# Batch 1 of an attention-and-FFN kernel: its second score group one place earlier, its state read one place earlier, its two weight transposes next to each other

## The chip, the cores and the metric

The kernel runs on one core of one Trainium2 chip. The metric is device time in microseconds (us) of one execution; the kernel before takes 153.98 us (median of five runs, 153.81 to 155.08). A separate execution was profiled. All times on the profile's clock are us from the start of the profiled span.

A core has five engines, each with its own instruction stream that is worked off in order: TensorE (PE: matmuls, with weight loads on their own row, PEld), VectorE (DVE), ScalarE (ACT), GpSimd (POOL) and SyncE (SP). Streams wait for each other on semaphores only. PE writes its results to PSUM; ACT and DVE copy them from there to SBUF. DMAs are started from an engine's stream and then run on their own; the starts by POOL, which also convert float32 to bf16 on the way, form one queue, those by SP and ACT another.

## The reference, cut to what matters

x is (8, 8, 512, 64): 8 batches, 8 heads, 512 rows, 64 features. state is (8, 8, 32, 64): 32 state rows per head. Attention is computed both ways, and its result goes through a feed-forward layer whose hidden value is the largest of three products.

```python
scores = scale * np.matmul(x, state.transpose(0, 1, 3, 2))   # 512 x 32 per head
a = softmax(scores, -1)
xread = np.matmul(a, state)                                  # 512 x 64 per head
scores2 = scale * np.matmul(state, x.transpose(0, 1, 3, 2))
sread = np.matmul(softmax(scores2, -1), x)                   # 32 x 64 per head
tokens = concatenate([xread, sread], axis=2)                 # 8 x 544 tokens of 512 features
h = np.maximum(np.maximum(tokens @ w1, tokens @ w2), tokens @ w3)   # 768 hidden
out = h @ w_out
```

## The kernel before, in words

The state is folded into the weights: for each batch the kernel forms G = state x W (W is w1, w2 and w3 side by side), so that the first FFN product of the xread tokens is a x G, with the softmax weights a (4 heads of 32 states fill the 128 rows of a matmul; the 8 heads make two such groups, g = 0 for the even heads and g = 1 for the odd ones). The sread tokens are gathered in a tile of their own and go through the FFN at the end.

Per batch b the steps are these; the lines are those of the profile.

- `x_transpose(b, g, ...)` (L178, L182): x is transposed on PE, and copied to `xT`.
- `scores(b, g0, g1)` (L200, L205): 8 matmuls per group into a PSUM tile `psh` and one exponential on ACT into `e`.
- `softmax(b, g0, g1, ...)` (L213, L215, L220): row sums `den` and reciprocals `rden` on DVE, then the product `a` on POOL.
- `sread(b)` (L267, L276, L278): 32 small matmuls of `e` with x into the PSUM tile `psr`, and two DVE operations, `rd` and `sr`.
- `a_transpose(b, g, copy)` (L231, L232): 4 PE transposes of `a` into the PSUM tile `pat`, and a copy to `aT` by the engine that is named, ACT or DVE.
- `g_cols(b, ms)` (L327, L333): for each 128 hidden columns m, 8 matmuls of a 64x32 block of the state with a slice of W, packed side by side in the array, into a PSUM tile `pg`, and an ACT copy to `G`. With `defer` the ACT copy is put off until after the `t` copy of the next `x_maxout`.
- `x_maxout(b, m)` (L377, L382, L385, L386): 6 matmuls (three products, two head groups each) into three PSUM tiles `pw`, an ACT copy `t` of the first, a DVE maximum `t` with the second, and a DVE maximum `ht` with the third.
- `ffn_out(b, j)` (L416, L419): 6 matmuls with w_out, an ACT copy, and a DMA to the output.

PSUM is kept in two rings: `two`, two tiles of two banks (`pg` among others), and `pw`, four tiles of one bank. `pw`, `psh`, `pxt` (the x transposes), `psr` and `pat` all take the next tile of the second ring in the order in which they are written down, so a step waits until the tile four places before it was read.

The schedule is written out by hand: the order of the calls is the order in each engine's stream. Batches 0 and 1 are woven into each other at the start, while the loads still run; from batch 2 on a loop places the steps of the next batch between the `x_maxout` steps of this one.

W is loaded by POOL in four slices of hidden columns (m = 0; m = 1; m = 2 and 3; m = 4 and 5), each in three parts, one per weight matrix (`load_w(c, parts)`, L109). All matmuls of `g_cols` for a column need all three parts of its slice. Between the calls that this document deals with POOL's stream holds, in this order: the product `a` of batch 1's group 0, the second part of the last slice, the product `a` of batch 1's group 1, the last part of the last slice (`load_w(3, (2,))`), the cast of states 2 and 3 to bf16 (L136, tile `st`), the loads of x of batch 2 (L70), of w_out (L471), of the other states (L58), of x of batches 3 and 4, and some fills. SP's stream holds, behind that cast, the DMA that transposes these states (L144, `stT`).

Of the kernel before, what the change touches and what calls it, by code (L numbers as in the profile page):

```python
# [15 lines left out]
def kernel(  # L16
# [14 lines left out]
    nc = tc.nc  # L31
# [10 lines left out]
    J = 4  # L42
# [11 lines left out]
    dve, act, pool = nc.vector.tensor_copy, nc.scalar.copy, nc.gpsimd.tensor_copy  # L54


    def load_st(k, eng):
        eng.dma_start(  # L58
            out=st_f[k],
            in_=state[2 * k:2 * k + 2].rearrange("b h n d -> (b h n) d").rearrange("(p t) d -> p t d", t=4))  # L60
# [38 lines left out]
    def m_cols(t, m):  # L99
        c = [m0 <= m < m1 for m0, m1 in chunks].index(True)  # L100
        f = (m - chunks[c][0]) * 128
        return w_slices(t, c)[:, :, :, f:f + 128]
# [27 lines left out]
    def bd(b, h):  # L130
        return bds[b // 2][:, b % 2, h]
# [18 lines left out]
    def states_place(k, copy):  # L150
        for c in range(2):
            r = slice(64 * c, 64 * c + 64)
            copy(out=bds[k][r, :, :, c, :].rearrange("p b h (q t) -> p (b h) q t", t=4),  # L153
                 in_=stT[k][r].rearrange("p t (k q) -> p k q t", q=8))
# [8 lines left out]
    def new(d, b, shape, name, bufs=2):  # L163
        d[b] = work.tile(shape, BF16, tag=name, bufs=bufs, name=name)
# [23 lines left out]
    def scores(b, g0, g1):  # L188
        n = g1 - g0
        if g0 == 0:  # L190
            new(e, b, [128, J, 2, HS, Ns], "e")
        if n == 2:
            p = pp.tile([128, J, n, HS, Ns], F32, tag="two", name="ps")
        else:
            p = pp.tile([128, J, n, HS, Ns], F32, tag="pw", bufs=4, name="psh")
        for jj in range(2):
            for g in range(g0, g1):
                for s in range(HS):
                    h = 2 * s + g
                    nc.tensor.matmul(  # L200
                        p[:, 2 * jj:2 * jj + 2, g - g0, s, :], xT[b][:, h, jj, :],
                        bd(b, h).rearrange("p c n -> p (c n)"),
                        start=(g == g0 and s == 0 and (n == 2 or jj == 0)),
                        stop=(g == g1 - 1 and s == HS - 1), skip_group_check=True)
        nc.scalar.activation(out=e[b][:, :, g0:g1], in_=p, func=AF.Exp, scale=scale)  # L205

    def softmax(b, g0, g1, *parts):

        n = g1 - g0
        if g0 == 0:  # L210
            new(a, b, [128, J, 2, HS, Ns], "a")
        den = work.tile([128, J, n, HS], F32, tag=f"den{n}", name="den")
        nc.vector.reduce_sum(out=den, in_=e[b][:, :, g0:g1], axis=AX.X)  # L213
        rden = work.tile([128, J, n, HS], F32, tag=f"rden{n}", name="rden")
        nc.vector.reciprocal(out=rden, in_=den)  # L215
        j0 = 0
        for mul, nj in parts:
            r = slice(j0, j0 + nj)
            j0 += nj
            mul(  # L220
                out=a[b][:, r, g0:g1].rearrange("p j g s n -> p j (g s) n"),
                in0=e[b][:, r, g0:g1].rearrange("p j g s n -> p j (g s) n"),
                in1=rden[:, r].rearrange("p j g s -> p j (g s)").unsqueeze(3).to_broadcast((128, nj, n * HS, Ns)))

    def a_transpose(b, g, copy):

        if g == 0:
            new(aT, b, [128, J, 2, 128], "aT", bufs=3)
        p = pp.tile([128, J, 128], BF16, tag="pw", bufs=4, name="pat")
        for j in range(J):  # L230
            nc.tensor.transpose(p[:, j, :], a[b][:, j, g].rearrange("p s n -> p (s n)"), ident)  # L231
        copy(out=aT[b][:, :, g, :], in_=p)  # L232
# [17 lines left out]
    def sread(b):  # L250


        padded = b >= 2
        p = pp.tile([128, 2, 2 * D], F32, tag="pw", bufs=4, name="psr")
        for j in range(J):
            for g in range(2):
                for s in range(HS):
                    h = 2 * s + g
                    if padded:
                        c0 = (2 * h + j // 2) * PW + 1 + (D + 1) * (j % 2)  # L260
                        cols = x_pads[b % 2][:, c0:c0 + D + 1]
                        c = slice(j % 2, D + 1 + j % 2)
                    else:
                        xj = xv[b][:, h, j, :]
                        cols = bass.AP(xj.tensor, xj.offset, (xj.ap[0], (XW - (h * J + j) * D, 2), (1, D)))
                        c = slice(0, 2 * D)
                    nc.tensor.matmul(  # L267
                        p[32 * s:32 * s + 32, g, c], e[b][:, j, g, s, :], cols,
                        start=(j == 0 and g == 0), stop=(j == J - 1), skip_group_check=True,
                        tile_position=(0, 32 * s))  # L270
        den, c = p[:, :, D:D + 1], slice(0, D)
        if padded:
            den, c = work.tile([128, 2, 1], F32, tag="rs", name="rs"), slice(1, D + 1)
            nc.vector.reduce_sum(out=den, in_=p[:, :, 0:D + 2:D + 1], axis=AX.X)
        rd = work.tile([128, 2, 1], F32, tag="rd", name="rd")
        nc.vector.reciprocal(out=rd, in_=den)  # L276
        sr = work.tile([128, 2, D], BF16, tag="sr", bufs=B, name="sr")
        nc.vector.tensor_mul(out=sr, in0=p[:, :, c], in1=rd.to_broadcast((128, 2, D)))  # L278
        late.append(lambda: nc.sync.dma_start_transpose(
            out=ats[:, b].rearrange("p s n -> p (s n)"), in_=sr.rearrange("p g d -> p (g d)")))  # L280
# [4 lines left out]
    def flush_copies():  # L285
        while copies_due:
            copies_due.pop(0)()
# [30 lines left out]
    def g_cols(b, ms, copies=(act, act), defer=(False, False)):  # L318
        flush_copies()
        for m, copy, wait in zip(ms, copies, defer):  # L320
            if m == 0:
                new(G, b, [128, 2, NM * 384], "G", bufs=3)
            p = pp.tile([128, 2, 512], F32, tag="two", name="pg")
            pv = p[:, :, 0:384].rearrange("p g (i f) -> p g i f", i=3)
            for s in range(HS):
                for g in range(2):
                    nc.tensor.matmul(  # L327
                        pv[32 * s:32 * s + 32, g], bd(b, 2 * s + g)[64 * g:64 * g + 64, g, :],
                        m_cols(w_sb, m)[64 * g:64 * g + 64, s],
                        start=True, stop=True, tile_position=(64 * g, 32 * s))  # L330

            def place(m=m, pv=pv, copy=copy):
                copy(out=m_cols(G[b], m), in_=pv)  # L333

            if wait:
                copies_due.append(place)
            else:
                place()
# [27 lines left out]
    def maxout(b, m, n, lhs, rhs, nk, mid=None):  # L366


        if m == 0:
            new(ht, b, [128, NM, n], "ht", bufs=4)  # L370
        pw = []
        for k0, k1 in ((0, nk),) if mid is None else ((0, 1), (1, nk)):
            for i in range(3):
                if k0 == 0:
                    pw.append(pp.tile([128, 512], F32, tag="pw", bufs=4, name=f"pw{i}"))
                for k in range(k0, k1):
                    nc.tensor.matmul(pw[i][:, 0:n], lhs(i, k), rhs(k), start=(k == 0), stop=(k == nk - 1))  # L377
            if k1 < nk:
                mid()
        t0 = work.tile([128, 512], BF16, tag="t0", name="t0")  # L380
        t1 = work.tile([128, 512], BF16, tag="t1", name="t1")
        nc.scalar.copy(out=t0[:, 0:n], in_=pw[0][:, 0:n])  # L382
        if copies_due:
            copies_due.pop(0)()
        nc.vector.tensor_max(t1[:, 0:n], t0[:, 0:n], pw[1][:, 0:n])  # L385
        nc.vector.tensor_max(ht[b][:, m, :], t1[:, 0:n], pw[2][:, 0:n])  # L386

    def x_maxout(b, m, mid=None):
        maxout(b, m, 512,
               lambda i, k: m_cols(G[b], m)[:, k, i],  # L390
               lambda k: aT[b][:, :, k, :], 2, mid)
# [68 lines left out]
    load_w(3, (1,))  # L460
    x_maxout(0, 0, lambda: x_transpose(1, 1, dve))
    load_st(1, nc.scalar)
    g_cols(0, (1,))
    g_cols(1, (0,), defer=(True,))
    scores(1, 1, 2)
    softmax(1, 1, 2, (nc.gpsimd.tensor_mul, J))
    load_w(3, (2,))
    states_cast(1, pool)
    states_transpose(1, True)
# [8 lines left out]
    for k in range(1, B // 2):  # L478
        nc.gpsimd.memset(bds[k], 0.0)
    states_place(1, pool)  # L480
    x_maxout(0, 1)
    sread(1)
    a_transpose(1, 0, act)
    g_cols(1, (1,))
    a_transpose(1, 1, dve)
    x_maxout(1, 0, lambda: None)
    g_cols(0, (2, 3), defer=(False, True))
    x_maxout(1, 1)
# [97 lines left out]
```

## Time and profile before

| | us |
|---|---|
| five timed runs | 153.81, 153.88, 153.98, 154.55, 155.08 |
| profiled execution: its own time | 154.74 |
| its span, first to last instruction | 152.9 |
| PE busy | 144.6 (95% of the span) |
| ACT busy | 94.0 (61%) |
| DVE busy | 97.8 (64%) |
| POOL busy | 66.5 (43%) |
| wait of PE for a part of W's second slice | 0.97, from 14.15 to 15.12 |
| wait of PE for the ACT copy of that slice's G (batch 0) | 0.42, up to 16.39 |
| wait of PE for `a` of batch 1, group 1 | 0.13, up to 19.17 |

How to read it. The page gives busy times per engine and a table of groups of like instructions. The timeline gives the instructions of a stretch: start, length, engine, line, operation, written and read tiles, shape, how many, and in square brackets the idle time before and what ended it. Two instructions of one engine may overlap by about 0.1 us, since the next starts while the last one drains. The chain of waits goes back from the last instruction to what released each step. Matmuls are pipelined: their lengths overlap, and what counts is the distance from one start to the next.

### The profile page before, as it was taken

To read this page: it belongs to the slowest core of one execution; us is meant where nothing else is said; L and a number is where in the kernel's file an instruction comes from. 1 tells how busy PE (TensorE), PEld (TensorE's weight loads), DVE (VectorE), ACT (ScalarE), POOL (GpSimd) and SP (SyncE) were. 2 spreads that over 40 slices of the span, in tenths; PEclk is the share of its full clock that TensorE was granted. 3 is DMA by queue.
4 is the path that set the end of the run, shared out by engine and by line. 5 is a ranking of instruction groups with operands and counts; after the bars stand their busy time and mean duration, and the time that the engine had idled before them with its cause. 6 is when DMAs were issued, how large, how long until landed. Compare 5 with 4: busy or idle time off the path is not lost.

```text
span 152.9 us, 3474 instructions
## 1 busy us (share of the span) xinstructions
PE 144.6 (95%) x1366; PEld 70.6 (46%) x1382; DVE 97.8 (64%) x177; ACT 94.0 (61%) x145; POOL 66.5 (43%) x80
## 2 busy tenths in 40 slices
PE   6987899999999999999999999999999999999990
PEld 2544443554453445344534453445344556665450
DVE  3488668768827685768576867776767684566010
ACT  3654788686848656865686568656865637332440
POOL 8998499836421782078307310821082100100410
PEclk9999999999999999999999999999999999999998
DMA  4999999999938999999585953071206120210473
GB/s 117 192 180 188 208 161 111 198 234 196 252 63 176 149 181 281 173 120 180 188 185 77 191 165 137 6 201 41 110 13 198 43 107 0 81 58 0 163 253 137
DMA packets 37520, 21.85 MB, mean 143 GB/s; under 512 B 22528, under 2 KB 35072, under 8 KB 37504
## 3 DMA queue, kind: packets, MB, share of 16 engines
q0 software_dynamic: 17184, 14.94, 54.2%
q1 hardware_dynamic: 20032, 6.43, 23.2%
q10 hardware_dynamic: 288, 0.26, 0.6%
q8 instruction: 11, 0.18, 0.5%
q14 instruction: 5, 0.04, 0.1%
HBM read 15.20 MB, written 8.91 MB: 158 GB/s over the span
## 4 chain that ended last, share of the span: by engine, by line
PE 82%; POOL 5%; DMA 5%; ACT 2%; issue 2%; DVE 1%; POOLq 0%; DVEq 0%
PE pw L377 43%; PE po L416 28%; DMA w<-in_moe_w_dram 5%; PE pg L301 4%; POOL w L109 2%; PE ps L200 2%; POOL x L80 2%; PE pg L327 1%; PE psr L267 1%; ACT G L333 1%; PE ph L408 1%; ACT t L382 1%; POOL a L220 1%; DVE t L385 0%; DVE den L213 0%
## 5 line engine op out<-in xcount | busy, mean ns | idle before, releaser
L377 PE MATMUL pw<-aT,G 128*128 128x512 bf16 x288 | 69.2, 379 | 0.4 <-ACT G L333 0.4
L385 DVE TENSOR_TENSOR t<-t,pw 128x512 bf16<-128x512 bf16 (+1 forms) x54 | 35.1, 649 | 29.0 <-ACT t L382 28.5
L416 PE MATMUL po<-wout,ht 128*128 128x512 bf16 x183 | 46.4, 379 | 1.0 <-DVE t L385 0.2
L377 PEld LDWEIGHTS <-G 128*128 128x128 bf16 x288 | 26.8, 98 | 32.0 <-issue 2.9
L386 DVE TENSOR_TENSOR ht<-t,pw 128x512 bf16<-128x512 bf16 (+1 forms) x54 | 35.5, 658 | 5.6
L382 ACT CAST t<-pw 128x512 bf16<-128x512 f32 (+1 forms) x54 | 30.5, 565 | 12.0 <-PE pw L377 11.2
L419 ACT COPY osb<-po 128x512 f32<-128x512 f32 x33 | 19.3, 586 | 28.5 <-PE po L416 28.5
L416 PEld LDWEIGHTS <-ht 128*128 128x128 bf16 x198 | 18.8, 98 | 24.0 <-issue 2.8
L430 POOL DMA_DIRECT2D out_dram<-osb x14 | 7.9, 567 | 47.8 <-ACT osb L419 42.0
L220 POOL TENSOR_TENSOR a<-e,rden 128x1024 bf16<-128x1024 bf16 (+2 forms) x10 | 15.3, 1533 | 26.3 <-DVE rden L215 16.7
L308 ACT CAST G<-pg 128x1024 bf16<-128x1024 f32 x24 | 24.5, 1021 | 2.3 <-PE pg L301 1.6
L246 POOL COPY xp<-x 128x2048 bf16<-128x2048 bf16 x6 | 11.3, 1883 | 0.0
L213 DVE TENSOR_REDUCE den<-e 128x32 f32<-128x1024 bf16 (+1 forms) x10 | 10.0, 997 | 2.0 <-ACT e L205 2.0
L333 ACT CAST G<-pg 128x768 bf16<-128x768 f32 x11 | 8.8, 808 | 2.6 <-PE pg L327 2.6
L109 POOL DMA_DIRECT2D w<-in_moe_w_dram x12 | 9.2, 782 | 0.3 <-DMA x<-in_x_dram 0.3
L377 PE MATMUL pw<-ats,w 128*128 128x256 bf16 x72 | 8.7, 272 | 0.0
L205 ACT ACTIVATE e<-ps 128x1024 bf16<-128x1024 f32 x6 | 6.2, 1029 | 3.7 <-PE ps L200 3.7
L377 PEld LDWEIGHTS <-w 128*128 128x128 bf16 x72 | 7.1, 98 | 1.9
L301 PE MATMUL pg<-w,bd 64*32 64x512 bf16 x192 | 7.5, 381 | 0.0
L127 PE MATMUL idle<-zero 128*128 128x512 bf16 x15 | 5.5, 506 | 1.3 <-DVE zero L85 1.2
L153 POOL COPY bd<-stT 64x512 bf16<-64x512 bf16 x6 | 6.5, 1079 | 0.6 <-DMA stT<-st 0.4
L200 PEld LDWEIGHTS <-xT 128*128 128x128 bf16 x128 | 4.9, 98 | 2.1 <-issue 0.3
(61 smaller groups left out, 85.7 us busy)
## 6 DMA issues: line engine op xcount, KB each, us to landing
out_dram<-osb POOLq DMA_DIRECT2D x14, 512.0 KB, 3.5
x<-in_x_dram POOLq DMA_DIRECT2D x6, 512.0 KB, 9.2
w<-in_moe_w_dram POOLq DMA_DIRECT2D x6, 256.0 KB, 6.8
x<-in_x_dram POOLq DMA_DIRECT2D x3, 256.0 KB, 6.2
w<-in_moe_w_dram POOLq DMA_DIRECT2D x6, 128.0 KB, 6.4
wout<-in_moe_w_out_dram POOLq DMA_DIRECT2D x1, 768.0 KB, 11.4
out_dram<-osb SPq DMA_DIRECT2D x3, 256.0 KB, 2.0
x0f<-in_x_dram SPq DMA_DIRECT2D x1, 512.0 KB
```

The costliest lines, as they stand in the source:

```text
L109: nc.gpsimd.dma_start(out=w_slices(w_sb, c)[:, :, i, :], in_=w[:, :, m0 * 128:m1 * 128])
L220: mul(out=a[b][:, r, g0:g1].rearrange("p j g s n -> p j (g s) n"), in0=e[b][:, r, g0:g1].rearrange("p j g s n -> p j (g s) n"), in1=rden[: ...
L246: nc.gpsimd.tensor_copy(out=x_pads[b % 2][:, 2:2 + 2 * H * PW].rearrange("p (k c) -> p k c", c=PW)[:, :, 0:2 * D], in_=x_sb[b][:, 0:XW].re ...
L301: nc.tensor.matmul(ps[g][32 * s:32 * s + 32], bd(b, 2 * s + g)[64 * g:64 * g + 64, g, :], w_sb[64 * g:64 * g + 64, s, c0:c1], start=True, ...
L308: copy(out=G[b][:, :, c0:c1], in_=p[:, :, 0:n])
L333: copy(out=m_cols(G[b], m), in_=pv)
L377: nc.tensor.matmul(pw[i][:, 0:n], lhs(i, k), rhs(k), start=(k == 0), stop=(k == nk - 1))
L382: nc.scalar.copy(out=t0[:, 0:n], in_=pw[0][:, 0:n])
L385: nc.vector.tensor_max(t1[:, 0:n], t0[:, 0:n], pw[1][:, 0:n])
L386: nc.vector.tensor_max(ht[b][:, m, :], t1[:, 0:n], pw[2][:, 0:n])
L416: nc.tensor.matmul(p, ht[b][:, m, j * 128:(j + 1) * 128], wout_sb[:, m, :], start=(m == 0), stop=(m == NM - 1))
L419: act(out=o[:, j, :], in_=p)
```

## The change

Three calls of batch 1 change their place, and one copy its engine.

1. `scores(1, 1, 2)` and `softmax(1, 1, 2, ...)` stand ahead of `g_cols(0, (1,))` and `g_cols(1, (0,))`, the two pieces of G that read W's second and first slice, and no longer behind them. On PE these are 8 matmuls that pass 16; on ACT the exponential passes the copy of `G` for batch 0, m = 1. On DVE, POOL and SP nothing passes anything by this.
2. `sread(1)` stands ahead of `x_maxout(0, 1)`, and no longer behind it: its 32 matmuls pass 6 on PE, and its two DVE operations pass the two maxima.
3. `a_transpose(1, 1)` stands right behind `a_transpose(1, 0)`, ahead of the piece `g_cols(1, (1,))`, and its copy is made by ACT and no longer by DVE: on PE 4 transposes pass 8 matmuls, DVE has one copy less, ACT one more.

The streams of POOL and SP hold the same instructions in the same order. The tiles of the `pw` ring are dealt in the new order.

```diff
     x_maxout(0, 0, lambda: x_transpose(1, 1, dve))
     load_st(1, nc.scalar)
+    scores(1, 1, 2)
+    softmax(1, 1, 2, (nc.gpsimd.tensor_mul, J))
     g_cols(0, (1,))
     g_cols(1, (0,), defer=(True,))
-    scores(1, 1, 2)
-    softmax(1, 1, 2, (nc.gpsimd.tensor_mul, J))
     load_w(3, (2,))
     states_cast(1, pool)
     states_transpose(1, True)
...
     states_place(1, pool)
+    sread(1)
     x_maxout(0, 1)
-    sread(1)
     a_transpose(1, 0, act)
+    a_transpose(1, 1, act)
     g_cols(1, (1,))
-    a_transpose(1, 1, dve)
     x_maxout(1, 0, lambda: None)
```

`x_maxout(1, 0, lambda: None)` is the form in which the three matmuls of head group 0 stand ahead of the three of group 1, so that only the last three need `aT` of group 1.

## The prediction

> **What bounds the kernel now.** I read the page's busy lines first, to see which engine fills the span.
>
> ```profile
> PE 144.6 (95%) x1366; PEld 70.6 (46%) x1382; DVE 97.8 (64%) x177; ACT 94.0 (61%) x145; POOL 66.5 (43%) x80
> ```
>
> PE is busy for 95% of the span, so only what shortens PE's idle time, or its work, can pay. The change leaves PE's work alone. Next the waits of PE, from 21 us to the end:
>
> ```profile
> PE pg L327 <- ACT G L333: 0.3, 1, 0.3
> PE po L416 <- DVE t L385: 0.2, 1, 0.2
> ```
>
> Behind 21 us PE waits only twice, each time for engines that PE itself feeds, and never for a DMA. So all that PE wins by 21 us should reach the end, unless a load becomes late. Third, the chain of waits in the stretch that the diff touches:
>
> ```profile
> 7.71 7.37 DMA w<-in_moe_w_dram
> 15.07 0.04 issue
> 15.12 0.40 PE pg L327 x8
> ...
> 15.54 0.80 ACT G L333
> 16.34 0.51 ACT e L205
> ...
> 18.07 1.05 POOL a L220
> ...
> 19.17 0.40 PE pat L231 x4
> ```
>
> The third part of W's second slice lands at 15.07 and releases the pieces of G; behind them come the copy of G, the exponential of batch 1's odd heads, its sums, its product, its transposes. The scores need nothing of W: they hang on this load by their place only. Last the timeline, PE first and then the others:
>
> ```profile
> 13.33 0.81 PE L377 MATMUL pw<-aT,G 128*128 128x512 bf16 x3
> 15.12 0.52 PE L327 MATMUL pg<-w,bd 64*32 64x384 bf16 x16 [0.97 <-DMA w<-in_moe_w_dram]
> 15.57 0.41 PE L200 MATMUL psh<-bd,xT 128*128 128x64 bf16 x8
> 16.39 1.47 PE L377 MATMUL pw<-aT,G 128*128 128x512 bf16 x6 [0.42 <-ACT G L333]
> 17.79 0.63 PE L267 MATMUL psr<-x,e 128*32 128x128 bf16 x32
> 18.35 0.40 PE L231 MATMUL pat<-ident,a 128*128 128x128 bf16 x4
> 18.68 0.36 PE L327 MATMUL pg<-w,bd 64*32 64x384 bf16 x8
> 19.17 0.40 PE L231 MATMUL pat<-ident,a 128*128 128x128 bf16 x4
> 19.42 1.46 PE L377 MATMUL pw<-aT,G 128*128 128x512 bf16 x6
> ```
>
> ```profile
> 13.84 0.63 DVE L182 COPY xT<-pxt 128x1024 bf16<-128x1024 bf16 x1
> 15.16 0.69 DVE L386 TENSOR_TENSOR ht<-t,pw 128x512 bf16<-128x512 bf16 x1
> 16.23 0.60 ACT L205 ACTIVATE e<-psh 128x512 bf16<-128x512 f32 x1
> 18.07 1.04 POOL L220 TENSOR_TENSOR a<-e,rden 128x512 bf16<-128x512 bf16 x1 [2.19 <-DVE rden L215]
> 18.79 0.59 ACT L232 COPY aT<-pat 128x512 bf16<-128x512 bf16 x1 [0.47 <-PE pat L231]
> 19.60 0.42 DVE L232 COPY aT<-pat 128x512 bf16<-128x512 bf16 x1
> ```
>
> The reader is to see two holes on PE, 0.97 and 0.42 us, with 0.41 us of scores and 0.63 us of state reads standing behind them.
>
> **The change, part by part.** The point to compare is the end of batch 1's first maxout group on PE, now 19.42 + 1.46 = 20.88, since all behind it keeps its order.
>
> *Scores into the first hole.* They need `xT`, whose copy ends at 13.84 + 0.63 = 14.47. A release costs 0.05 (from 15.07 to 15.12), so they start at 14.52 and end 0.41 later, at 14.93, 0.14 ahead of the load. The exponential runs from 14.97 to 15.57. The copy of G started at 15.54. ACT starts the next instruction 0.1 before the last one ends (the exponential at 16.23, the copy's end at 16.34), so it could take this copy from 15.47: no loss. PE's next maxout group then stays at 16.39. The cover is thin: an exponential later by more than 0.07 delays that group one for one.
>
> *Softmax.* DVE is free at 15.16 + 0.69 = 15.85. With the old distances (sums at 16.87, product at 18.07 to 19.11) the product would run from 17.05 to 18.09, 1.02 earlier.
>
> *State read into the second hole.* Its 32 matmuls start behind the pieces of G, at about 15.57 where the scores stood, and end at 15.62 + 0.63 = 16.25, once the exponential is in. That is before 16.39, so they cost nothing; covered by the wait for the copy of G, and 0.56 (17.79 to 18.35) if that wait were gone. Its `rd` and `sr` come behind the reciprocals on DVE, which end at 16.89, and end near 17.4, before DVE's next maximum can start (the ACT copy `t` ends at 17.62).
>
> *Transposes.* The maxout group ends its issue at 17.79 as now; the first transposes start there rather than at 18.35, and are done at 18.19. The second ones wait for the product: 18.09 + 0.05 = 18.14. Then the 8 matmuls of G 0.33 later (18.35 to 18.68), at 18.47. ACT's deferred copy of G runs from 17.52 to 18.32, so the first `aT` copy runs from 18.22 to 18.81, the second 0.48 behind it (18.79 to 19.27 was the distance), from 18.70 to 19.29.
>
> *What is late next.* The next maxout group can start at 18.81 + 0.05 = 18.86. Its second PSUM tile is the one that `ht` of the group before still reads: `t` starts at 17.65 on DVE and `ht` 0.79 behind it (the distance in later pairs, 21.11 to 21.90), ending at 19.13, so the second matmul starts at 19.18. The other four follow by 0.216 each (1.46 less 0.38, over five). The sixth starts at 20.04 and ends at 20.42. The group's second half needs `aT` by 19.61 and has it at 19.34. So 20.88 becomes 20.42: **0.46 us won**.
>
> *The moved copy.* ACT takes 0.59 for what DVE did in 0.42. The slower copy lies 0.27 off the path; ACT's next copies, of G at 19.18 and of `t` at 20.0, still meet theirs. If that cover were gone it would cost 0.17.
>
> *Queues.* POOL's issues behind the product, and SP's transpose of the states behind POOL's cast, come up to 1.02 earlier. The cast's input lands at 13.76 + 5.0 = 18.76, the cast would start at 18.85, so it holds nothing up. The last part of W was issued at 19.07 and landed 5.7 later, at 24.8; its reader stands at 25.88, now at 25.42. The load of x of batch 2 landed at 28.6, its reader's weight load stands at 29.17, now 28.71: enough even if that load gained nothing. w_out (21.31 + 11.4 = 32.7) is read at 34.08, now 33.6. From both sides: between nothing (all loads ahead of need, as the waits behind 21 us say) and, in the nearest row of a late load, the wait of 0.97. I take nothing.
>
> The Trainium skill, page "DMA: Bandwidth & Descriptors", section "Anatomy of one DMA — SWDGE (gpsimd) path", gives a POOL-issued transfer about 2.0 us and its bytes over 436e3; for 256 KB that is an estimate of 2.6 us, against the 5.7 measured here. By it the last part of W would be there near 20.7, and the sum would still be 0.46. The same page, "SWDGE vs HWDGE vs iDMA", says that the two kinds of queue are served in turn, which speaks against moving the state transpose nearer to the W loads; by it alone the sum would only shrink, by an amount that the page doesn't give. The row behind that:
>
> ```profile
> 22.00:23.00 1.00, 1.00 (x6) 0.41 (x5) 1.00 (x2) 1.00 (x3) 1.00 (x3) 1.00 1.57 200
> 23.00:24.00 1.00, 1.00 (x6) 0.29 (x3) 0.90 (x3) 0.82 (x2) 1.00 (x2) 1.00 1.31 51
> ```
>
> The last column is GB/s: it falls from 200 to 51 a few us behind the issue of the transpose.
>
> Sum: the profiled execution, 154.74 (span 152.9 and 1.84 around it), would be 154.28. The median of the timed runs lies 0.76 below it; less 0.46 it is **153.5**.
>
> **The rivals.** *W's second slice lands earlier in the timed runs.* For it: the profiled run is 0.76 slower than the median, and in this stretch every step of before hangs on the landing at 15.07; against it: the time could as well be lost around the span. If it lands at L, the old end moves with it, 20.88 - (15.07 - L). The new one stops moving at L = 15.0, where ACT's exponential holds the copy of G: 20.35. They meet at L = 14.54. Below that the change loses; at L = 14.1, when PE is only just free (its last matmul starts at 13.77), it loses 0.44: 154.4. This is the slower mechanism with the weaker price.
>
> *The state transpose starves the last part of W.* For it: the fall to 51 GB/s, now 1.02 earlier and so over that load. Against it: the load is also issued 1.02 earlier, and in the old order landed amid the transposes. The new order loses nothing until 25.42, and ends slower than before from a landing at 25.88. Say it is held until the transposes' traffic ends, about 25.1 (an estimate: the transpose lands 28.2 now, its traffic is over near 26), and that half of the part ahead of it and all of its own are still to move, at the 1.3 per part that lie between landings now: it lands at 27.0, a stall of 1.6, net 1.1 slower, 155.1.
>
> *Timed runs wait for loads that the profile shows as early.* For it: two of five runs are 0.6 and 1.1 slower than the rest; against it: no such wait behind 21 us. Then the loads' 1.02 counts where PE's 0.46 does: 153.0.
>
> *The scores don't fit.* If `xT` were late by over 0.14, the pieces of G wait for them, at most their 0.41: 153.5 to 153.9.
>
> **How the numbers follow.** I take 0.5% (0.77 us) as what a measurement here can tell from no change. The forecast, with the misfit of scores within it, gets 0.55, at 153.1 to 153.9 (own range); a fifth of that lies below 153.21. Loads that were late: 0.15, faster. An early W slice: 0.15, nearly all within 0.5%. A starved last part: 0.15, two thirds of it beyond 154.75, and I give 0.03 more to slower for the early slice with the copy's 0.17 on top. Faster 0.11 + 0.15 = 0.26; slower 0.10 + 0.03 = 0.13; within 0.61. The range of 152.8 to 154.7 takes in the loads' gain with 0.2 to spare, the early slice to its end, and the milder part of the starved load.
>
> **What would show it.** Right: scores on PE at about 14.5, the wait for W at about 0.2 or less, state reads inside the wait for the copy of G, the product ending near 18.1, the maxout group of batch 1 ending near 20.4, and the same two small waits later. Wrong: the copy of G behind a late exponential; a PE wait for w at 25 or for x at 29; `t` copies later than their matmuls by more than before. It would be wrong altogether if the landing at 15.07 is not what the timed runs have, or if the moved loads collide.

## The result and the profile after

The changed kernel takes 154.29 us (median of 54 runs, 153.9 to 155.17). The kernel before, run many more times beside it, takes 154.18 us (94 runs, 153.4 to 156.05). The ratio is 1.0012, with a 95% interval of 1.0004 to 1.0020: slower by 0.06 to 0.31 us, where 0.46 us of gain was forecast. Runs more than 1.5% above the fastest run of the same kernel are left out of the ratios here and below, which leaves three of six and five of nine runs of the two kernels with a late slice.

The profiled execution of the changed kernel took 154.72 us, its span is 152.8. On the page PE is as busy as before, and DVE has given one copy to ACT:

```profile
PE 145.0 (95%) x1366; PEld 70.7 (46%) x1382; DVE 97.3 (64%) x176; ACT 94.4 (62%) x146; POOL 66.2 (43%) x80
```

The waits of PE from 21 us to the end are those of before, one for one:

```profile
PE pg L327 <- ACT G L333: 0.3, 1, 0.3
PE po L416 <- DVE t L385: 0.2, 1, 0.2
```

The timeline of PE in the stretch of the change (start, length, operation, shape, count, idle time before):

```profile
13.72 0.81 PE L377 MATMUL pw<-aT,G 128*128 128x512 bf16 x3
14.91 0.41 PE L200 MATMUL psh<-bd,xT 128*128 128x64 bf16 x8 [0.38 <-DVE xT L182]
15.25 0.52 PE L327 MATMUL pg<-w,bd 64*32 64x384 bf16 x16
15.70 0.88 PE L267 MATMUL psr<-x,e 128*32 128x128 bf16 x32
16.70 1.47 PE L377 MATMUL pw<-aT,G 128*128 128x512 bf16 x6
18.00 0.83 PE L231 MATMUL pat<-ident,a 128*128 128x128 bf16 x8
18.76 0.36 PE L327 MATMUL pg<-w,bd 64*32 64x384 bf16 x8
19.16 1.46 PE L377 MATMUL pw<-aT,G 128*128 128x512 bf16 x6
```

Batch 1's first maxout group ends at 19.16 + 1.46 = 20.62, 0.26 before the old 20.88. But there is no wait for W any more, for a reason that has nothing to do with the change: W's second slice is there early. The DMA view gives, for that load's third part, issued at 7.85, 6.5 us to landing (14.36); in the profile of before it was issued at 7.71 and took 7.4 (15.07). And PE came to the place 0.39 later than in the profile of before, because x of batch 0 had landed later (6.82 against 6.46). The scores now wait for `xT`, and the chain of waits in this stretch starts there and no longer at a load:

```profile
14.31 0.56 DVE xT L182
14.86 0.05 issue
14.91 0.42 PE psh L200 x8
15.33 0.02 issue
15.35 0.60 ACT e L205
15.95 0.70 ACT G L333
16.65 0.05 issue
16.70 0.62 PE pw L377 x2
```

The reader is to see the copy of G behind the exponential: it starts at 15.85, 0.1 before the exponential ends, though its slice has been there since 14.36.

```profile
15.85 0.79 ACT L333 CAST G<-pg 128x768 bf16<-128x768 f32 x1
```

A second thing is in the timeline of DVE. One maximum near 32 us starts 0.51 after the instruction before it, and not 0.11 after it as its twin did before (32.22, behind an end at 32.12). First before, then after:

```profile
31.44 0.68 DVE L385 TENSOR_TENSOR t<-t,pw 128x512 bf16<-128x512 bf16 x1
32.22 0.69 DVE L386 TENSOR_TENSOR ht<-t,pw 128x512 bf16<-128x512 bf16 x1
```

```profile
31.17 0.68 DVE L385 TENSOR_TENSOR t<-t,pw 128x512 bf16<-128x512 bf16 x1
32.36 0.69 DVE L386 TENSOR_TENSOR ht<-t,pw 128x512 bf16<-128x512 bf16 x1 [0.51 <-PE pxt L178]
```

Its two inputs were ready: `t` at 31.85, and the last matmul of its `pw` group at 31.02. The bracket names the x transposes on PE, which end at 32.21, since they are the last thing that ended before it. But the maximum does not need them: its twin before starts at 32.22 while they run until 32.48 (31.86 + 0.62). PE's maxout group behind it takes 1.64 instead of 1.46 (the transposes and that group on PE, first before, then after):

```profile
31.86 0.62 PE L178 MATMUL pxt<-ident,x 128*128 128x128 bf16 x8
32.32 1.46 PE L377 MATMUL pw<-aT,G 128*128 128x512 bf16 x6
```

```profile
31.59 0.62 PE L178 MATMUL pxt<-ident,x 128*128 128x128 bf16 x8
32.05 1.64 PE L377 MATMUL pw<-aT,G 128*128 128x512 bf16 x6
```

So 0.26 won at 20.6 are 0.09 at 34.0 (34.08 before, 33.99 now).

Two questions follow. Does W's second slice land near 15.1, or is that a chance of one execution? And whose is the 0.17 at 32 us?

Three numbers of each profile answer them. *Lateness*: from the end of the copy of `xT` of batch 1's odd heads to the landing of the third part of W's second slice. *Front*: from that end of the copy to the end of batch 1's first maxout group. *Tail*: from there to the end of the span.

### The profile page after: what moved, and what is told of

Same layout as the page of the kernel before. It is cut to its first block, busy times and chain, and to the rows that moved or that the text cites. A ratio compares the mean times of both kernels' runs of the same rounds, so it can differ in the third digit from the quotient of the medians.

```text
span 152.8 us, 3476 instructions
## 1 busy us (share of the span) xinstructions
PE 145.0 (95%) x1366; PEld 70.7 (46%) x1382; DVE 97.3 (64%) x176; ACT 94.4 (62%) x146; POOL 66.2 (43%) x80
## 4 chain that ended last, share of the span: by engine, by line
PE 84%; ACT 4%; DVE 4%; DMA 4%; issue 2%; POOL 0%; POOLq 0%; DVEq 0%
PE pw L377 44%; PE po L416 28%; PE pg L301 4%; DMA x<-in_x_dram 4%; PE ps L200 2%; PE psr L267 1%; ACT G L333 1%; DVE den L213 1%; PE pg L327 1%; ACT e L205 1%; ACT t L382 1%; PE ph L408 1%; DVE a L220 1%; PE pxt L178 1%; PE psh L200 1%
## 5 line engine op out<-in xcount | busy, mean ns | idle before, releaser
L127 PE MATMUL idle<-zero 128*128 128x512 bf16 x15 | 6.1, 547 | 1.3 <-DVE zero L85 1.2
```

## The experiments

Each ratio is against the kernel before in the same session.

**Both kernels once more.** No edit.

> The kernel before, profiled once more. Theory A (landing): the landing of W's second slice at 15.07 in the first profile is a chance of that execution; most executions have it near 14.4, as the profile of the changed kernel has (14.36). Then this profile shows the slice landing at 14.2 to 14.6, PE's wait for it at 0.3 us or less, and batch 1's first maxout group ending on PE near 20.3 and not at 20.88. Theory B (lost later): the landing is near 15.1 in each execution of before, the hole of about 1 us is there again, the group ends near 20.9, and what the change wins by then is lost behind it. Time: the same as before, ratio 0.998 to 1.002, under both.

> The changed kernel, profiled once more, beside the kernel before. Under theory A its group end does not follow the landing of the slice below 15.0: near 20.4 to 20.7 wherever the slice lands, set by the copy of xT, the exponential and then the copy of G. Under theory B the group ends near 20.4 and a PE wait of 0.2 to 0.5 us appears behind it that before does not have. Ratio to before 1.000 to 1.003 under both.

Before again: 154.19 us, ratio 1.0016 (1.0001 to 1.0032) to the same program in that session; the interval just misses one, which shows what a thousandth is worth here. So it is not certain that the changed kernel, at 1.0012, is truly slower; it is certain that the forecast gain of 0.46 us (0.003) is absent. Its PE timeline:

```profile
13.09 0.81 PE L377 MATMUL pw<-aT,G 128*128 128x512 bf16 x3
14.48 0.52 PE L327 MATMUL pg<-w,bd 64*32 64x384 bf16 x16 [0.58 <-DMA w<-in_moe_w_dram]
14.93 0.41 PE L200 MATMUL psh<-bd,xT 128*128 128x64 bf16 x8
15.76 1.47 PE L377 MATMUL pw<-aT,G 128*128 128x512 bf16 x6 [0.42 <-ACT G L333]
```

The slice lands at 14.44, lateness 0.23 where the first profile had 0.60; the hole is 0.58 and not 0.97, and the group ends at 20.25. I had expected at most 0.3 of hole under the landing theory, so this profile lies between the two theories; it shows that the 15.07 did not repeat. The changed kernel again: 154.40 us, ratio 1.0021 (1.0000 to 1.0043), lateness 0.24, front 5.77, exactly as in its first profile at a lateness of -0.49. In this second profile the slice lands at 14.98, nearly as late as the 15.07, but the copy of `xT` ends late too, at 14.74: what counts is the one against the other. Its tail is 132.20, that of before 132.01.

**The scores alone.**

```diff
     load_st(1, nc.scalar)
+    scores(1, 1, 2)
+    softmax(1, 1, 2, (nc.gpsimd.tensor_mul, J))
     g_cols(0, (1,))
     g_cols(1, (0,), defer=(True,))
-    scores(1, 1, 2)
-    softmax(1, 1, 2, (nc.gpsimd.tensor_mul, J))
```

> Only the scores and their softmax stand ahead of the pieces of G; the state read and the transposes stay where before has them. Theory A: with the slice there at 14.4 the scores delay the copy of G by their exponential, about 0.5 us, the state read's 0.6 us comes behind the maxout group again, and the earlier product ends no wait: slower than before by 0.3 to 0.8 us, ratio 1.002 to 1.005. Theory B: the hole takes the scores, the maxout group starts as before, the product's wait of 0.13 goes: faster or the same, ratio 0.997 to 1.000.

154.67 us, ratio 1.0045 (1.0027 to 1.0062). Slower, as the landing theory has it. PE's wait for the copy of G, 0.42 before, is 0.93 here, and the state read stands behind it as before:

```profile
14.49 0.52 PE L327 MATMUL pg<-w,bd 64*32 64x384 bf16 x16
15.94 1.47 PE L377 MATMUL pw<-aT,G 128*128 128x512 bf16 x6 [0.93 <-ACT G L333]
17.34 0.63 PE L267 MATMUL psr<-x,e 128*32 128x128 bf16 x32
```

Front 6.33 at a lateness of -0.03; tail 132.01.

**State read and transposes alone.**

```diff
+    sread(1)
     x_maxout(0, 1)
-    sread(1)
     a_transpose(1, 0, act)
+    a_transpose(1, 1, act)
     g_cols(1, (1,))
-    a_transpose(1, 1, dve)
```

> Only the state read is moved ahead of batch 0's second maxout group, and the second transposes behind the first, with their copy on ACT; the scores stay behind the pieces of G. The state read now waits for the exponential, which comes behind the copy of G, and the maxout group stands behind it. Theory A: with the slice at 14.4 the exponential ends near 16.1, the maxout group starts at 16.6 to 16.7, where before starts it near 15.7: a loss of about 0.4 to 0.7 us against before, about equal to the changed kernel, ratio 1.000 to 1.005. Theory B: with the slice at 15.1 the exponential ends at 16.84, the group starts at 17.3 rather than at 16.4, and the transposes wait for the product: ratio 1.003 to 1.008.

154.99 us, ratio 1.0073 (1.0050 to 1.0095): slower than the landing theory allowed. Lateness 0.45, front 6.70, tail 132.18. PE stands 0.75 inside the state read, until the exponential that now comes behind the copy of G:

```profile
15.39 0.24 PE L267 MATMUL psr<-x,e 128*32 128x128 bf16 x4
16.38 0.57 PE L267 MATMUL psr<-x,e 128*32 128x128 bf16 x28 [0.75 <-ACT e L205]
16.89 1.47 PE L377 MATMUL pw<-aT,G 128*128 128x512 bf16 x6
```

So either half of the change, made alone, loses. The scores need the state read in their shadow, and the state read needs the scores ahead of it.

**The slice late on purpose, in both orders.** The third part of W's second slice is issued one place later.

```diff
-    load_w(1)
-    load_w(2, (0,))
+    load_w(1, (0, 1))
+    load_w(2, (0,))
+    load_w(1, (2,))
```

> The kernel before with the third part of W's second slice loaded behind the first part of the third slice, so that it lands about one part later (1.35 us behind 14.4, so 15.7), and nothing else moved. Theory A: a wait of PE for the slice of 1.0 to 1.7 us in this profile, the maxout group of batch 1 ending 1.3 later than with an early slice, and the kernel slower than before by 0.7 to 1.3 us, ratio 1.005 to 1.009. Theory B (before always waits for the slice, which lands near 15.1): slower by 0.6 or less, ratio up to 1.004.

> The changed kernel with the same later part of W. Theory A: here the hole that the change fills is real, so this one beats the one with the same late part in the old order by 0.3 to 0.6 us: ratio to the kernel before 1.002 to 1.006, and 0.002 to 0.004 below the old order with the late part. Theory B: what is won is lost behind it also here: the two late ones differ by less than 0.001.

Old order 156.22 us (median of three runs), ratio 1.0116 (1.0064 to 1.0169); new order 155.32 us (median of five), ratio 1.0075 (1.0041 to 1.0109). The part came later than I had meant (lateness 2.11 and 2.43), and both lose more than expected. The new order is ahead by 0.004, as the landing theory expects and at the upper end of its range, but the intervals overlap, and all runs spread over three microseconds (154.81 to 158.62 and 154.45 to 157.61). So the timed runs do not settle this pair. In the new order's profile PE waits 2.01 for the slice with the scores done ahead of it:

```profile
14.30 0.41 PE L201 MATMUL psh<-bd,xT 128*128 128x64 bf16 x8 [0.38 <-DVE xT L183]
16.72 0.52 PE L328 MATMUL pg<-w,bd 64*32 64x384 bf16 x16 [2.01 <-DMA w<-in_moe_w_dram]
17.17 0.63 PE L268 MATMUL psr<-x,e 128*32 128x128 bf16 x32
18.00 1.47 PE L378 MATMUL pw<-aT,G 128*128 128x512 bf16 x6 [0.20 <-ACT G L334]
```

That maxout group starts 1.32 behind the landing, as it does in every profile of the old order that waited for the slice. From there to the end of batch 1's first maxout group it is 3.92 us, against 4.49 in the two first profiles of the old order: 0.57 won where the slice is late. (In the old order's late profile that stretch can't be compared, because its clock fell; see the last section.)

**The slice early on purpose, in both orders.**

```diff
-    load_w(0)
+    load_w(0, (0, 1))
+    nc.vector.memset(w_slices(w_sb, 0)[:, :, 2, :], 0.0)
     load_heads(1, 1)
```

> The kernel before without the load of the third weight's part of W's first slice (zeros are written in its place, so that product is left out of the maximum for the first 128 hidden columns), so that all later loads land about 0.7 us earlier and the second slice is there before PE is free. Theory A: no wait of PE for the slice, group end near 20.2 or earlier, ratio to the kernel before 0.996 to 0.999. Theory B: the hole shrinks from 1 us to 0.3, ratio 0.995 to 0.997.

> The changed kernel without the same load (zeros in place of the third weight's part of W's first slice). Theory A: the scores have no hole to fill and only delay the copy of G, so this one is slower than the old order without that load by 0.3 to 0.6 us: 0.002 to 0.004 above its ratio, and near 1.000 to 1.002 against the kernel before, as the changed kernel itself. Theory B: the two differ by less than 0.001.

Old order 153.92 us, ratio 0.9980 (0.9959 to 1.0000); new order 154.10 us, ratio 0.9997 (0.9979 to 1.0014). Both kernels leave out the third weight's product for the first 128 hidden columns. The slice is there 1.35 and 1.12 ahead of `xT`. No wait for W is left in either, and the old order is ahead: fronts 5.38 and 5.77 in the profiles, tails 132.01 and 132.02. (The zeros are written by DVE, which has one instruction more by it; why that bears on the tail is in the next experiment.) The gap of the timed runs, 0.0017, is a little less than the 0.002 to 0.004 I had expected, and the intervals overlap. So it is the profiles that show the difference turn with the landing, late against early, as the landing theory demands; the timed runs agree in sign and prove it for neither pair.

**The late maximum at 32 us: one DVE instruction more, and one less.** The change takes one copy from DVE. To the changed kernel a small fill is added at the start, and in the kernel before only the engine of that copy is changed.

```diff
     nc.vector.memset(bds[0], 0.0)
+    more = const.tile([128, 1], BF16, name="more")
+    nc.vector.memset(more, 0.0)
```

```diff
-    a_transpose(1, 1, dve)
+    a_transpose(1, 1, act)
```

> The changed kernel with one instruction more on DVE, a fill of 128 single values at the start, so that DVE's stream has as many instructions in front of batch 2 as before has. In the profiles so far the stretch from the end of batch 1's first maxout group to the end of the span is 132.0 us where the order of before holds behind it, and 132.17 to 132.2 in the changed kernel and two relatives: there one DVE maximum near 32 us starts 0.4 late with its inputs ready, and PE loses 0.17. Theory S (place in the stream): the late start belongs to a place in DVE's stream, which the missing copy shifted by one; then it is gone here, the stretch is 132.0, and the ratio to before is 0.998 to 1.001. Theory R (the new order of state read and transposes does it): the stretch stays at 132.17 to 132.2, ratio 1.000 to 1.003.

> The kernel before with only the copy of the second transposes moved from DVE to ACT; no call changes its place. Theory S: DVE's stream is one instruction shorter, so the late maximum near 32 us appears and the stretch behind batch 1's first maxout group is 132.17 to 132.2; with the ACT copy behind the copy of G, the group itself ends up to 0.5 later; ratio to before 1.001 to 1.005. Theory R: the stretch stays at 132.0, ratio 1.000 to 1.004.

With the fill: 154.24 us, ratio 1.0006 (0.9991 to 1.0020), front 5.77, tail 132.04. With the copy alone: 154.66 us, ratio 1.0040 (1.0023 to 1.0058), tail 132.18. The timeline of DVE, with the fill:

```profile
30.89 0.68 DVE L387 TENSOR_TENSOR t<-t,pw 128x512 bf16<-128x512 bf16 x1
31.68 0.69 DVE L388 TENSOR_TENSOR ht<-t,pw 128x512 bf16<-128x512 bf16 x1
```

and with the copy alone, nothing else being moved:

```profile
31.02 0.68 DVE L385 TENSOR_TENSOR t<-t,pw 128x512 bf16<-128x512 bf16 x1
32.20 0.69 DVE L386 TENSOR_TENSOR ht<-t,pw 128x512 bf16<-128x512 bf16 x1 [0.51 <-PE pxt L178]
```

The late start comes with the shorter stream and goes with the longer one, whatever the order of the calls. The copy on ACT also costs in front: there it waits behind the copy of G, and PE stands 0.38 in the middle of batch 1's first maxout group. Front 5.92 at a lateness of -0.54, where the order of before has 5.38 (the floor that its early-slice profile shows).

**Two variants.** One makes the deferred copy of batch 1's first G at once, into ACT's idle 0.70 ahead of `t`, on top of the fill; the other adds the fill to the kernel with only state read and transposes moved.

```diff
-    g_cols(1, (0,), defer=(True,))
+    g_cols(1, (0,))
```

> The changed kernel with the small DVE fill at the start and with the copy of batch 1's first G made at once, ahead of the copy t on ACT, rather than put off behind it. ACT is idle for 0.70 us there in the changed kernel (16.64 to 17.34), so the copy of 0.80 fits nearly; the first copy of the transposes then starts as soon as they are done. From the copy of xT to the end of batch 1's first maxout group: 5.77 us in all profiles of the changed order so far; here 5.65 to 5.72. In the order of before it is 5.81 plus the lateness of the W slice behind the copy of xT, and 5.39 at least. If those lie evenly about zero, this one is at 0.998 to 1.000 of before. If the gain doesn't show, 5.77 stays and the ratio is that of the changed kernel with the fill alone, 1.0006.

> State read and transposes moved as in the changed kernel, the scores left behind the pieces of G, and the small DVE fill at the start. Without the fill this was 1.0073 of before, while its profile accounts for 0.44 us in front (6.70 us from the copy of xT to the group's end at a lateness of 0.45, where before would have 6.26) and 0.17 behind: 0.61 us, 1.004. If the profile tells all, the fill takes the 0.17 away: stretch behind the group 132.0, ratio 1.002 to 1.004. If the timed runs lose at a place that this profile didn't show, the ratio stays above 1.005.

The first: 154.19 us, ratio 1.0011 (0.9995 to 1.0026). Its front is 5.67 and its tail 132.03, as expected, and yet the timed runs show no gain over the fill alone; a tenth of a microsecond is below what they can tell. The second: 154.46 us, ratio 1.0029 (1.0012 to 1.0046), inside its range; front 5.82 at a lateness of -0.51, tail 132.02. The fill explains 0.17 of the 0.7 us between this kernel and its twin without it. What the rest was is not settled.

**All profiles in one table.**

| kernel | lateness | front | tail |
|---|---|---|---|
| before | 0.60 | 6.42 | 132.03 |
| before again | 0.23 | 6.04 | 132.01 |
| before, slice early | -1.35 | 5.38 | 132.01 |
| before, slice late (clock at half for 3.4 us) | 2.11 | 9.53 | 132.01 |
| changed | -0.49 | 5.77 | 132.19 |
| changed again | 0.24 | 5.77 | 132.20 |
| changed, slice early | -1.12 | 5.77 | 132.02 |
| changed, slice late | 2.43 | 7.67 | 132.17 |
| changed, with fill | -0.18 | 5.77 | 132.04 |
| changed, with fill, copy of G at once | 0.17 | 5.67 | 132.03 |
| scores alone | -0.03 | 6.33 | 132.01 |
| state read and transposes alone | 0.45 | 6.70 | 132.18 |
| state read and transposes alone, with fill | -0.51 | 5.82 | 132.02 |
| copy alone | -0.54 | 5.92 | 132.18 |

Two readings. The old front is 5.81 plus the lateness (6.42 - 0.60 = 5.82, 6.04 - 0.23 = 5.81), down to 5.38; the new one is 5.77 for any lateness up to 0.24 that was seen. They cross near -0.04. Where the slice is late the new front moves too: 7.67 at 2.43 is 5.24 plus the lateness. If it rises one for one, as the old one does, it leaves 5.77 at 0.53; no profile lies between 0.24 and 2.43.

A hint of the same is in the timed runs. The middle half of the 94 runs of before lies within 0.45 us (153.97 to 154.42), that of the 54 runs of the changed kernel within 0.27 (154.24 to 154.51), as befits one end that moves with the landing and one that doesn't. It is no more than a hint: the old order with the early slice, whose end should not move, spreads as widely in its 12 runs (153.32 to 154.60).

## Why the prediction was wrong, point by point

**The step that failed** is the first of the parts, "Scores into the first hole", and in it the 15.07 at which W's second slice lands: I took one execution's landing, 0.60 behind `xT`, for that of the kernel. The ten profiles whose loads up to that slice are unchanged have latenesses of 0.60, -0.49, 0.23, 0.24, -0.03, 0.45, -0.18, -0.54, 0.17 and -0.51, in the order of this document: about zero on average. The first profile has the largest of all. The sign was there to see before: the profiled run, at 154.74, was 0.76 above the median of the five, and it is slower than 84 of the 94 runs now known.

**The rival that came true** is the first one, "W's second slice lands earlier in the timed runs". Its form held: the old end moves with the landing and the new one does not; it put the crossing at a lateness of 0.07 (14.54 less 14.47), and the profiles have it at -0.04. I gave it 0.15 because I set the 0.76 against the time around the span. But the span is where it was: it moves with the time, 152.9 at 154.74, 152.4 at 154.27 and 152.0 at 153.81, and the time around it stays near 1.8 to 1.9.

**The sizes.** Put the ten latenesses into the old front (5.81 plus lateness, at least 5.38): 6.41, 5.38, 6.04, 6.05, 5.78, 6.26, 5.63, 5.38, 5.98 and 5.38, on average 5.83. The new front is 5.77 in nine of these cases and, by the line through the late slice, 5.84 in the first. So the change wins 0.05 in front on average, where 0.46 was forecast, and 0.57 in an execution like the first profile. Then the tail takes 0.17. That leaves it 0.12 slower, an estimate from ten profiles; measured are 0.11 between the medians and 0.06 to 0.31 by the ratio. The 154.29 lies inside the 152.8 to 154.7 that I had stated, but only in part for a reason that I had given: the early slice was among the rivals, the 0.17 was not.

**The moved copy** was costed at nothing, with ACT's and DVE's next work as its cover. On ACT that held in the changed order. On DVE the copy that went cost 0.17, by a late start 12 us further on, at a place that no row of before shows. Nothing in the prediction looked for that.

**State read into the second hole** held: it starts at 15.70 and ends at 16.58, before the copy of G lets the maxout group go at 16.70, and costs nothing. The scores-only kernel shows the price where it has no cover. **What is late next** was half right: the first matmul of batch 1's group does wait for the first `aT` copy (19.11, start 19.16), but the wait for `ht` at the second matmul was not there, and the front is 5.77 rather than the 5.95 (20.42 less 14.47) that the sum has. The second matmul starts at 19.38, before that `ht` ends at 19.44, so the tile that `ht` reads was not the second one. That is 0.10 of the 0.18; for the rest, batch 0's second maxout group starts 1.85 behind `xT`, with no wait for the slice, and not 1.92 (16.39 less 14.47).

**Softmax** and **Queues** held. The product ends at 18.38, 3.53 behind `xT` (predicted 3.62). The last part of W, issued at 18.34, landed 5.9 later; x of batch 2 landed at 27.57 against 28.66. No PE wait for a load appears behind 21 us in any profile of the changed order, so the state transpose starved nothing, and loads that come earlier pay nothing either. On the page "DMA: Bandwidth & Descriptors" of the Trainium skill, the estimate of 2.6 us for such a part of W is not met here: no part of W took under 5.2 us in any profile.

**The scores don't fit** was costed at up to 0.41, for a late `xT`. That is the same race seen from its other side, and it was the usual case rather than the exception: what counts is the slice against `xT`, and both move by some tenths from run to run.

## What to carry to other kernels

When a hole ends with a load, take its length from several executions, or bound it by the spread of the timed runs; a profiled run well above the median is a warning that its waits are longer than usual. Work put ahead of a load pays only as far as the load is late behind that work's own input; where the load is early, the same work delays what the load would have released. And an order that takes work off one wait may need all its parts: here each half alone lost 0.3 to 0.7%.

## What the runs showed of the hardware that I had not expected

A DVE instruction can start 0.4 us late with its inputs ready, and here the number of instructions ahead of it decided whether it did. With one DVE instruction fewer in front, the maximum at 32 us started 0.49 to 0.51 behind the end of its forerunner in all five such profiles (the changed kernel, twice, with the late slice, with state read and transposes alone, with the copy alone); with the old number or one more it did so in none of nine. What the engine waits for there was not tried. That it is the fetch of its instruction stream is only a guess, and the traces do not speak for it: in none of the five does a transfer of the instruction queues begin between 26 and 35 us.

The landings of the same loads differ from run to run by more than half a microsecond: the third part of W's second slice between 13.94 and 15.07 in the ten profiles with unchanged loads ahead of it, x of batch 0 between 6.17 and 6.82. That is about the spread of the timed runs.

In the old order with the late slice PE idled 2.47 us (14.85 to 17.32), and from 18.6 to 22.0 us its granted clock fell to half; the maxout group took 2.74 in place of 1.47. In the new order, with the scores in between, the longest idle was 2.01 and the clock stayed full in the profiled execution. That was not so in every execution: over the span the clock was 0.984 to 0.989 in four of the old order's six runs and in four of the new order's nine, and 0.995 to 1.000 in the others, which are the shorter ones in both. The windows of the old order (last three columns: granted clock, DMA share, GB/s):

```profile
18.00:20.00 2.00, 1.58 (x11) 0.64 (x8) 0.82 (x2) 1.38 (x3) 0.00 (x0) 0.66 1.38 219
20.00:22.00 2.00, 2.00 (x35) 0.89 (x34) 1.42 (x3) 0.96 (x2) 1.72 (x2) 0.50 0.67 90
```

The page "TensorE: Matmul & The Clock Gate" of the Trainium skill, section "Part 1: The HAM clock gate (the "warmup" mystery)", says that the clock falls after an idle window of about 3.4 us. Here 2.47 us without a matmul, then 0.9 us of matmuls and another 0.42 without, was followed by it, so in this trace a shorter pause was enough.
